# Rows of V with their ones column at a pitch of 272 bytes instead of 260 in a fused attention and MLP kernel

One core of a Trainium2 chip. The metric is the device time of one execution in microseconds (us); lower is better.

## The reference, cut to what matters

```python
h = _layernorm(x) * (1 + ca) + sa                 # x: 1 x 2048 x 512
q = (h @ wq) -> 32 heads of 128                   # 8 KV heads, 4 query heads share one
scores = einsum('bhqd,bhkd->bhqk', q, k) * Dh ** -0.5
p = softmax(scores)                               # over 2048 keys
o = einsum('bhqk,bhkd->bhqd', p, v) @ wo
x = x + ga * o
...                                               # then a gated MLP with a spatial product
```

## The kernel before

Attention works on units: one KV group g (8) and one tile j of 128 queries (16). Scores are made transposed, keys on partitions, so that the exponentials can serve as weights (the stationary operand) of the product with V ("PV") without a transpose. V's rows carry a column of ones behind their 128 values; the 129th output column is then the softmax denominator.

```python
DV = DH + 2                                   # 130 elements of bf16: a pitch of 260 bytes
def load_v(g, rows, engine):
    v1 = late.tile([P, NKT, DV], BF16, name="v1")      # NKT = 16 rows in each partition
    nc.gpsimd.memset(v1[:, :, DH:DV], 1.0)             # the ones
    engine.dma_start(out=v1[:, :, 0:DH], in_=rows[:, g])
...
def qk(u, i):                                 # "QK": two matmuls of 512 columns, then the exponential
    ...
    nc.scalar.activation(out=pTs[u][:, 2 * i : 2 * i + 2, :], in_=s_ps..., func=ACT.Exp, scale=...)
...
def pv(u, i):                                 # eight matmuls a call
    ...
    if i % (2 * per) == 0:                    # two heads share one PSUM bank, DV floats apart
        o_pss[u] = bank("o_ps")[:, 0 : 2 * DV].rearrange("p (h d) -> p h d", h=2)
    for kt in range(part * NKT // per, (part + 1) * NKT // per):
        nc.tensor.matmul(
            o_ps[:, hh % 2, 0 : DH + 1],
            lhsT=pTs[u][:, kt, hh * P : (hh + 1) * P],
            rhs=groups[g]["v1"][:, kt, 0 : DH + 1],    # the moving operand: 129 columns of row kt
            start=(kt == 0), stop=(kt == NKT - 1),
        )
...
for it in range(NU + 6):                      # software pipeline: QK of unit it, PV of unit it - 1
    for i in range(NSLOT):                    # 8 "slots" a unit
        qk(it, i); pv(it - 1, i); ...         # and one 512-column matmul of a projection as filler
```

## Time and profile before

| | before |
|---|---|
| median time | 1361.92 us (3 runs, 1361.52 to 1363.76) |
| TensorE (PE) busy | 1318.9 us, 97% of the span |
| ScalarE (ACT) busy | 1079.6 us, 79% |
| attention, first PV to end of the last | 28.3 to 1173.0 us |
| one slot: 8 PV, 2 QK, 1 filler | 1115 ns, 1024 of them |

The prediction shows the lines. In the page's groups a line reads: source line, engine, operation, output<-input, shape, count | busy us, mean ns of one | idle us just before. Matmul records are pipelined and overlap, so the mean duration of a matmul (220 ns for 129 columns) is not what it costs. What it costs is the distance from its start to the start of the next, called its step below.

### The profile page before, as it was taken

How to read it: one execution, taken by the hardware profiler on the slowest of the kernel's cores; microseconds unless marked ns; L12 is line 12 of the kernel's file. 1: busy time of each engine (PE TensorE's matmuls, PEld its weight loads, DVE VectorE, ACT ScalarE, POOL GpSimd, SP SyncE). 2: the span in 40 equal slices, each digit the busy share in tenths (PEclk: the TensorE clock that was granted, in tenths of full speed). 3: DMA queues.
4: the chain of work that ended last, by engine and by line, in shares of the span. 5: the costliest groups of instructions: out<-in, count | busy, mean ns of one | idle time of the engine just before them, and what ended most of it. 6: DMA issues, size and time to landing. Idle time of an engine off the chain costs nothing.

```text
span 1360.8 us, 27642 instructions
## 1 busy us (share of the span) xinstructions
PE 1318.9 (97%) x12137; PEld 873.7 (64%) x12345; DVE 476.7 (35%) x1171; ACT 1079.6 (79%) x1059; POOL 45.5 (3%) x88
## 2 busy tenths in 40 slices
PE   6999999999999999999999999999999999979997
PEld 4666666666666666666666666666666667634444
DVE  5442222222222222222222222222222566872444
ACT  4789999999999999999999999999999999541000
POOL 1010000000000000000000000000000000110000
PEclk9999999999999999999999999999999999989999
DMA  8120021102211120022010310121111121143200
GB/s 270 28 63 16 13 63 36 21 17 33 62 21 21 32 67 17 16 36 66 17 17 17 83 21 17 18 66 32 21 20 17 25 32 32 25 108 78 67 23 26
DMA packets 141183, 56.53 MB, mean 42 GB/s; under 512 B 131104, under 2 KB 136352, under 8 KB 141056
## 3 DMA queue, kind: packets, MB, share of 16 engines
q1 hardware_dynamic: 137504, 42.17, 14.8%
q0 software_dynamic: 3408, 12.45, 3.6%
q8 instruction: 98, 1.61, 0.5%
q14 instruction: 29, 0.24, 0.1%
q10 hardware_dynamic: 144, 0.07, 0.0%
HBM read 21.63 MB, written 2.10 MB: 17 GB/s over the span
## 4 chain that ended last, share of the span: by engine, by line
PE 93%; DVE 3%; SPq 2%; issue 1%; DMA 1%; POOL 0%; ACT 0%; ACTq 0%; POOLq 0%; DVEq 0%
PE o_ps L901 35%; PE s_ps L879 35%; PE misc L843 7%; PE misc L933 6%; PE misc L1205 6%; PE s_ps L1100 2%; SPq L1012 1%; PE o_ps L1220 1%; PE s_ps L1064 1%; DMA wq_g<-in_A_wq_dram 1%; DVE stz L1081 1%; PE misc L796 0%; PE s_ps L1220 0%; DVE hT L803 0%; DVE z L679 0%
## 5 line engine op out<-in xcount | busy, mean ns | idle before, releaser
L886 ACT ACTIVATE pT<-s_ps 128x1024 bf16<-128x1024 f32 x1024 | 1046.0, 1024 | 106.5 <-PE s_ps L879 30.3
L901 PEld LDWEIGHTS <-pT 128*128 128x128 bf16 x8192 | 559.6, 98 | 241.8
L901 PE MATMUL o_ps<-v,pT 128*128 128x129 bf16 x8192 | 646.3, 220 | 0.0
L879 PE MATMUL s_ps<-qT,kT 128*128 128x512 bf16 x2048 | 609.4, 379 | 10.9 <-DVE qT L852 0.8
L912 DVE RECIPROCAL rall<-o_ps 128x2 f32<-128x2 f32 x256 | 43.6, 170 | 765.3 <-PE o_ps L901 765.2
L879 PEld LDWEIGHTS <-kT 128*128 128x128 bf16 x2048 | 196.7, 97 | 121.2 <-issue 1.5
L843 PE MATMUL misc<-hT,wq_g 128*128 128x512 bf16 (+2 forms) x462 | 169.1, 376 | 0.8 <-DMA wq_g<-in_A_wq_dram 0.8
L933 PE MATMUL misc<-wo_g,oT 128*128 128x512 bf16 x386 | 145.7, 377 | 0.0
L913 DVE TENSOR_TENSOR onorm<-o_ps,rall 128x256 bf16<-128x256 f32 x256 | 108.7, 425 | 8.8
L1205 PE MATMUL misc<-wsp,z 128*128 128x512 bf16 (+2 forms) x555 | 100.5, 336 | 1.9 <-DVE gb L1214 1.4
L852 DVE CAST qT<-misc 128x512 bf16<-128x512 f32 (+1 forms) x129 | 87.3, 676 | 1.7 <-PE misc L843 1.7
L1205 PEld LDWEIGHTS <-z 128*128 128x128 bf16 x560 | 50.6, 98 | 50.4 <-issue 1.9
L946 DVE TENSOR_TENSOR xacc<-misc,xacc 128x512 f32<-128x512 f32 x112 | 76.2, 680 | 0.0
L843 PEld LDWEIGHTS <-wq_g 128*128 128x128 bf16 x528 | 52.2, 100 | 4.0 <-issue 1.5
L933 PEld LDWEIGHTS <-oT 128*128 128x128 bf16 x512 | 50.3, 98 | 0.7
L1214 DVE TENSOR_TENSOR gb<-misc,bsp_bc 128x512 bf16<-128x512 f32 (+2 forms) x35 | 20.4, 584 | 60.9 <-PE misc L1205 60.9
L1100 PE MATMUL s_ps<-hT,win_sb 128*128 128x512 bf16 x109 | 27.2, 408 | 7.3 <-ACT z1T L1108 7.1
L1108 ACT ACTIVATE z1T<-s_ps 128x1024 bf16<-128x1024 f32 x14 | 14.2, 1024 | 20.1 <-PE s_ps L1100 11.6
L1064 PE MATMUL s_ps<-win_sb,hT 128*128 128x448 bf16 x128 | 27.0, 352 | 0.1
L1074 ACT ACTIVATE z<-s_ps 128x896 bf16<-128x896 f32 x16 | 14.7, 917 | 15.0 <-PE s_ps L1064 15.0
L1100 PEld LDWEIGHTS <-win_sb 128*128 128x128 bf16 x112 | 11.6, 103 | 22.5 <-issue 11.0
L712 POOL MEMSET v<- 128x32 bf16 x8 | 1.0, 127 | 715.7 <-issue 615.0
(68 smaller groups left out, 288.8 us busy)
## 6 DMA issues: line engine op xcount, KB each, us to landing
v<-in_A_v_cache_dram POOLq DMA_DIRECT2D x7, 512.0 KB, 6.7
wo_g<-in_A_wo_dram POOLq DMA_DIRECT2D x7, 512.0 KB, 4.8
wq_g<-in_A_wq_dram POOLq DMA_DIRECT2D x7, 512.0 KB, 6.0
wsp<-in_w_mod_dram SPq DMA_DIRECT2D x1, 2048.0 KB, 9.3
oT<-onorm SPq DMA_TRANSPOSE x128, 2.4
out_dram<-yout SPq DMA_DIRECT2D x15, 128.0 KB, 1.7
win_sb<-in_B_w_in_dram SPq DMA_DIRECT2D x1, 1792.0 KB, 13.7
wmod_a<-in_w_mod_dram SPq DMA_DIRECT2D x1, 1024.0 KB, 5.5
```

The costliest lines, as they stand in the source:

```text
L843: nc.tensor.matmul(ps[0][:, o0 : o0 + n], lhsT=wqs[g][:, dt, hh * DH : (hh + 1) * DH], rhs=hTs[ch][:, dt, c0 : c0 + n], start=(dt == 0), s ...
L852: nc.vector.tensor_copy(out=qTs[b][:, hs[0] : hs[-1] + 1, c0 : c0 + n], in_=ps[0][:, 0 : len(hs) * n].rearrange("p (h q) -> p h q", q=n),)
L879: nc.tensor.matmul(s_ps[:, h * 512 : (h + 1) * 512].rearrange("p (r q) -> p r q", r=REP), lhsT=groups[g]["kT"][:, kt * P : (kt + 1) * P], ...
L886: nc.scalar.activation(out=pTs[u][:, 2 * i : 2 * i + 2, :], in_=s_ps[:].rearrange("p (k q) -> p k q", k=2), func=ACT.Exp, scale=inv_sqrt_dh,)
L901: nc.tensor.matmul(o_ps[:, hh % 2, 0 : DH + 1], lhsT=pTs[u][:, kt, hh * P : (hh + 1) * P], rhs=groups[g]["v1"][:, kt, 0 : DH + 1], start=( ...
L912: nc.vector.reciprocal(out=rall[:, c0 : c0 + 2], in_=o_ps[:, :, DH])
L913: nc.vector.tensor_tensor(out=onorms[u][:, hh - 1 : hh + 1, :], in0=o_ps[:, :, 0:DH], in1=rall[:, c0 : c0 + 2].unsqueeze(2).to_broadcast([ ...
L933: nc.tensor.matmul(X_ps[:], lhsT=oTs[u][:, hh, :], rhs=groups[g]["wo"][:, hh, :], start=(hh == 0), stop=(hh == REP - 1),)
L946: nc.vector.tensor_tensor(out=xaccs[j][:], in0=X_ps[:], in1=xaccs[j][:], op=ALU.add)
L1064: nc.tensor.matmul(ps[0][:, hf * 512 : hf * 512 + FC], lhsT=h2Ts[j // CT][:, dt, (j % CT) * P : (j % CT + 1) * P], rhs=win_sb[:, dt, FH + ...
L1100: nc.tensor.matmul(ps[0][:, k * 512 : (k + 1) * 512], lhsT=win_sb[:, dt, f * P : (f + 1) * P], rhs=h2Ts[2 * ch2 + k][:, dt, :], start=(dt ...
L1205: nc.tensor.matmul(g_ps[:, :n], lhsT=z2[:, st, f * P : (f + 1) * P], rhs=wsp[t][:, st, c0 : c0 + n], start=(st == 0), stop=(st == NT - 1),)
```

## The change

Its intent: let every row of V begin at a multiple of 16 bytes. The same constant also spaces the two heads in PSUM (520 to 544 bytes) and widens the memset of the ones.

```diff
-    DV = DH + 2
+    DV = DH + 8
```

## The prediction

> **What bounds the kernel now.** I read the page first (busy shares, slices, costliest groups), then the windows, to see whether TensorE ever stops, then the timeline of one period, and last the start times of single matmuls.
>
> ```profile
> PE 1318.9 (97%) x12137; PEld 873.7 (64%) x12345; DVE 476.7 (35%) x1171; ACT 1079.6 (79%) x1059; POOL 45.5 (3%) x88
> ...
> L886 ACT ACTIVATE pT<-s_ps 128x1024 bf16<-128x1024 f32 x1024 | 1046.0, 1024 | 106.5 <-PE s_ps L879 30.3
> L901 PEld LDWEIGHTS <-pT 128*128 128x128 bf16 x8192 | 559.6, 98 | 241.8
> L901 PE MATMUL o_ps<-v,pT 128*128 128x129 bf16 x8192 | 646.3, 220 | 0.0
> L879 PE MATMUL s_ps<-qT,kT 128*128 128x512 bf16 x2048 | 609.4, 379 | 10.9 <-DVE qT L852 0.8
> ```
>
> TensorE is busy for 97% of the span. The third group, L901, is the product of the probabilities with V: 8192 matmuls that stream one row of V and its ones column, 129 columns of bf16. The changed pitch is the pitch of exactly that operand. The engine was never idle in front of it (0.0). ScalarE, which computes the exponentials (L886), has the second largest load.
>
> ```profile
> 300.00:600.00 300.00, 297.28 (x2912) 204.34 (x2961) 79.92 (x201) 275.52 (x270) 5.58 (x8) 1.00 0.16 33
> 600.00:900.00 300.00, 297.32 (x2913) 204.33 (x2961) 79.92 (x201) 275.52 (x270) 6.87 (x10) 1.00 0.17 34
> ```
>
> These are windows (length, then busy us and count of PE, PEld, DVE, ACT, POOL, then the granted clock and DMA). In attention, PE is busy 99% of the time at full clock, so whatever one matmul gives up shortens the run by itself.
>
> ```profile
> 600.70 0.63 PE L901 MATMUL o_ps<-v,pT 128*128 128x129 bf16 x8
> ...
> 601.16 0.38 PE L843 MATMUL misc<-hT,wq_g 128*128 128x512 bf16 x1
> ...
> 601.38 0.59 PE L879 MATMUL s_ps<-qT,kT 128*128 128x512 bf16 x2
> ...
> 601.81 0.63 PE L901 MATMUL o_ps<-v,pT 128*128 128x129 bf16 x8
> ...
> 1352.34 1.06 PE L1205 MATMUL misc<-wsp,z 128*128 128x128 bf16 x16
> ```
>
> The timeline (start, length, both in us) shows one period, a "slot": 8 PV matmuls, one 512-column matmul of filler, 2 QK matmuls, and 1.11 us later the next 8. There are 8192/8 = 1024 slots, and 1024 x 1.115 = 1142 us is the attention stretch of 28 to 1173 us. Eight PV matmuls take 0.63 us, of which the last one's modelled pipeline is 0.22 (the mean on the page), so seven steps take 0.41: 58.6 ns a step. The last line is my control: 16 matmuls of 128 columns from rows that all start at a multiple of 16 bytes, each with its own weight load as well: (1.06 - 0.22)/15 = 56.0 ns a step. One column more would account for 0.4 ns of the difference of 2.6.
>
> So I took the start of every PV matmul from the trace and sorted the steps by the index kt of the V row (means of 512 each; kt 7 and 15 end a slot, and the median of theirs is 59 to 60):
>
> ```
> kt          0    1    2    3    4    5    6  |   8    9   10   11   12   13   14
> kt*260 %16  0    4    8   12    0    4    8  |   0    4    8   12    0    4    8
> step, ns  56.7 60.9 59.1 59.1 55.9 59.3 59.2 | 56.7 60.9 59.2 59.1 55.9 59.1 59.3
> ```
>
> The period is four, and it is that of 260 modulo 16. The V tile starts at a multiple of 32 bytes in the built program, so rows with kt a multiple of 4 start at a multiple of 16 bytes. Those are the fast ones.
>
> **What the Trainium skill says.** "TensorE: Matmul & The Clock Gate", section "Back-to-back issue gap", gives the isolated gap of a warm matmul as N/2.4 + 2.5 ns: 56.25 for 129 columns. The trace agrees for aligned rows (56.7 and 55.9, mean 56.3) and for 512 columns (215.8 by the formula, 215 measured); unaligned rows take about 3 ns more. The same section states a sustained 81 ns for N=128 with weight loads; this trace does not agree (56 for the control, 59 for PV). "SBUF — State Buffer", section "Specifications (TRN2)", says that lines are of 16 bytes and that crossing to a new line costs something. A row of 258 bytes touches 17 lines at offset 0, 4, 8 or 12 alike, so the page points at 16 bytes but does not by itself give this cost. Its section "Operand start alignment" says its alignment rule "is about legality, not speed"; the trace shows that here there is a speed too.
>
> **The change part by part.** No instruction is added, removed or moved: the order of each engine is the same, and only the shapes of the 8 memsets differ.
>
> (a) Pitch of V, 260 to 272 bytes. 272 is 17 x 16, and the tile's base in the changed program is again a multiple of 32, so all 16 rows start as kt 0, 4, 8 and 12 do now. A slot's eight steps now: 56.7 + 60.9 + 59.1 + 59.1 + 55.9 + 59.3 + 59.2 and 59.5 into the next matmul (mean of those steps) = 469.7 ns. After: 8 x 56.25 = 450.0. Saved: 19.7 ns a slot, all on the engine that sets the end; 1024 slots give 20.2 us. The coarse reading agrees: (58.6 - 56.4) x 8192 = 18 us.
>
> (b) What takes part of it back. In the last four tiles of attention (1133 to 1165 us) four of eight slots have no filler; there the exponentials start every 904 ns, against 430 + 470 = 900 ns of PE work, so ScalarE is level with PE. Those 16 slots may save nothing: 16 x 19.7 = 0.3 us lost.
>
> (c) The same constant sets the pitch of the two heads in PSUM, 520 to 544 bytes. I expect nothing: the step is the same for both heads of a bank now (kt 0: 56.8 and 56.7), though the second starts at byte 520.
>
> (d) Memsets of V's tail grow from 128x32 to 128x128 elements. Eight of 0.13 us each, on POOL, which is 3% busy and fills V tens of us ahead: nothing on the path. Writes of V rows by DMA: the same sizes, and 14.8% + 3.6% of DMA share now.
>
> (e) After attention nothing changes; it starts 20 us earlier. Sum: 1361.9 - 20.2 + 0.3 = 1342.0 us, 1.5% less.
>
> **The rivals.**
>
> 1. ScalarE becomes the bound. For: 1024 ns of activation in a slot of 1115, which will be 1095, and 79% busy. Against: where nothing holds it back it starts every 904 ns, its records overlapping; its queue starts 1114 apart now because PE does. It would have to floor at 1100 to take a quarter of the gain (1347 us). I give that 4%.
>
> 2. Weight loads become the bound. For: each PV matmul has a load of 98 ns, and fast steps now come one in four, so a slow neighbour might lend it time. Against: the control sustains 56 ns for 16 matmuls in a row with a load each. Should loads hold the average at 57.5, the gain is halved (1352 us). 5%.
>
> 3. The period of four has another cause. The weights of PV lie 1024 bytes apart in kt, which also repeats after four where 4096 counts. Against: these addresses move by 256 bytes from head to head, and the pattern does not; all of them are multiples of 16. Then the change does nothing: 1362 us. 6%.
>
> 4. A row at a multiple of 16 ends with one element alone on its seventeenth line, and the skill wants two hits a line. But the fast rows of today end in just that way.
>
> 5. PSUM banks, operands or loads come too late for a faster PE. Loads of V, wq and wo land in 5 to 7 us and are issued tens of us early. QK needs a score bank that ScalarE has read: two slots of 1095 = 2190 ns against 0.59 + 1.02 plus hand-overs. No bind.
>
> **Range and chances.** The main case carries about 85%; within it the step may settle at 55.9 (23 us saved, 1339) or 56.7 (16.5 us, 1345). Repeats of before spread over 2.2 us. Range for 8 in 10: 1337 to 1349. Over 2% faster needs 27 us, that is 3.3 ns from each of 8192 matmuls, to 55.4 ns a step, below 129/2.4 + 2.5: 3%. Nothing got slower in the program: 1%. Within 2%: 96%.
>
> **What would show it right or wrong.** Right: eight PV matmuls in 0.61 us in the timeline (7 x 56.25 + 218); L901's busy time at 1024 x 0.612 = 627 us; its spread of durations narrower than 217/220/223, with the median near 218; exponentials 1095 ns apart; ScalarE's idle time up by some 20 us, and its busy time the same; the end of PV at about 1153 us instead of 1173; the MLP part as long as before. Wrong: a pattern of four in kt that stays (rival 3), equal steps at 57 to 59 (rival 2), or fast PV steps with new idle time in front of QK (rival 1 or 5).

## The result

| | before | changed |
|---|---|---|
| median, us | 1361.72 (4 runs) | 1347.0 (4 runs, 1346.54 to 1349.33) |
| ratio | | 0.9893, 95% interval 0.9875 to 0.9910 |
| slot, mean | 1115.2 ns | 1100.8 ns |
| end of the last PV matmul | 1172.98 us | 1158.12 us |
| from there to the end | 187.8 us | 187.1 us |

A ratio is the mean time of one kernel's fast runs over that of the other's of the same rounds, so not quite the ratio of the medians. The time lies in the predicted range, the change is within 2% as forecast, and the place is the predicted one: of 15.5 us by which the profiled span fell, 14.9 were gone by the end of PV.

The page of the changed kernel, the same groups as in the prediction:

```profile
PE 1303.1 (97%) x12137; PEld 860.4 (64%) x12345; DVE 476.3 (35%) x1171; ACT 1079.2 (80%) x1059; POOL 46.4 (3%) x88
...
L886 ACT ACTIVATE pT<-s_ps 128x1024 bf16<-128x1024 f32 x1024 | 1045.6, 1024 | 92.2 <-PE s_ps L879 16.5
L901 PEld LDWEIGHTS <-pT 128*128 128x128 bf16 x8192 | 548.5, 98 | 241.2
L901 PE MATMUL o_ps<-v,pT 128*128 128x129 bf16 x8192 | 631.4, 220 | 0.0
L879 PE MATMUL s_ps<-qT,kT 128*128 128x512 bf16 x2048 | 609.9, 379 | 10.8 <-DVE qT L852 0.8
```

L901 lost 14.9 us of busy time (646.3 to 631.4). The other matmul groups are as they were, ScalarE is as busy as before in a shorter span, and PE still never waits in front of PV. The windows of the changed kernel, columns as before (length, then PE, PEld, DVE, ACT, POOL):

```profile
300.00:600.00 300.00, 297.32 (x2950) 203.59 (x3000) 81.12 (x204) 279.13 (x274) 7.11 (x10) 1.00 0.16 33
600.00:900.00 300.00, 297.32 (x2949) 203.49 (x2998) 81.12 (x204) 279.15 (x273) 7.26 (x10) 1.00 0.18 34
```

PE is as busy as before (297.3 of 300 us), and gets 2950 matmuls done where it got 2912. A busy share could not have told this gain; a count does. The timeline of the changed kernel, successive slots:

```profile
600.76 0.62 PE L901 MATMUL o_ps<-v,pT 128*128 128x129 bf16 x8
...
601.86 0.62 PE L901 MATMUL o_ps<-v,pT 128*128 128x129 bf16 x8
...
602.96 0.62 PE L901 MATMUL o_ps<-v,pT 128*128 128x129 bf16 x8
```

Eight PV matmuls take 0.62 us (0.63 before) and slots start 1.10 us apart. The view of line L901 by itself (duration ns min/median/max), first of before, then of the changed kernel, shows that all of them have become alike:

```profile
L901 PE MATMUL o_ps<-v,pT x8192: 217/220/223, 28.3 to 1172.8; 128*128 128x129 bf16 x200
```

```profile
L901 PE MATMUL o_ps<-v,pT x8192: 218/220/220, 28.1 to 1157.9; 128*128 128x129 bf16 x200
```

The starts of single matmuls, from the trace, give the mean step of each of a slot's eight positions (KV group 2), and of the 512-column matmuls:

```
position      0    1    2    3    4    5    6    7  | 512 columns | slot
before      56.7 60.8 59.2 59.2 55.8 59.3 59.3 59.5 |   215.24    | 1115.4
changed     56.7 56.7 56.7 56.7 56.7 56.7 56.7 56.7 |   215.83    | 1100.8
```

So all eight are now equal, as predicted, but at 56.67 ns and not at 56.25; and the 512-column matmuls have become 0.6 ns slower each. Both are looked into below.

### The profile page after: what moved, and what is told of

The parts are those of the page before. It is cut to its first block, busy times and chain, and to the rows that moved or that the text cites. A ratio compares the mean times of both kernels' runs of the same rounds, so it can differ in the third digit from the quotient of the medians.

```text
span 1345.2 us, 27642 instructions
## 1 busy us (share of the span) xinstructions
PE 1303.1 (97%) x12137; PEld 860.4 (64%) x12345; DVE 476.3 (35%) x1171; ACT 1079.2 (80%) x1059; POOL 46.4 (3%) x88
## 4 chain that ended last, share of the span: by engine, by line
PE 92%; DVE 3%; SPq 2%; issue 1%; DMA 1%; POOL 0%; ACT 0%; ACTq 0%; POOLq 0%; DVEq 0%
PE s_ps L879 35%; PE o_ps L901 34%; PE misc L843 7%; PE misc L933 6%; PE misc L1205 6%; PE s_ps L1100 2%; SPq L1012 1%; PE o_ps L1220 1%; PE s_ps L1064 1%; DMA wq_g<-in_A_wq_dram 1%; DVE stz L1081 1%; DVE hT L803 0%; PE s_ps L1220 0%; PE misc L796 0%; DVE bnst L690 0%
## 5 line engine op out<-in xcount | busy, mean ns | idle before, releaser
L886 ACT ACTIVATE pT<-s_ps 128x1024 bf16<-128x1024 f32 x1024 | 1045.6, 1024 | 92.2 <-PE s_ps L879 16.5
L901 PEld LDWEIGHTS <-pT 128*128 128x128 bf16 x8192 | 548.5, 98 | 241.2
L901 PE MATMUL o_ps<-v,pT 128*128 128x129 bf16 x8192 | 631.4, 220 | 0.0
L879 PEld LDWEIGHTS <-kT 128*128 128x128 bf16 x2048 | 199.8, 98 | 120.1 <-issue 1.3
L1108 ACT ACTIVATE z1T<-s_ps 128x1024 bf16<-128x1024 f32 x14 | 14.2, 1024 | 19.5 <-PE s_ps L1100 10.9
L1074 ACT ACTIVATE z<-s_ps 128x896 bf16<-128x896 f32 x16 | 14.7, 917 | 14.9 <-PE s_ps L1064 14.9
```

The lines of the kernel that those rows point to most:

```text
L879: nc.tensor.matmul(s_ps[:, h * 512 : (h + 1) * 512].rearrange("p (r q) -> p r q", r=REP), lhsT=groups[g]["kT"][:, kt * P : (kt + 1) * P], ...
L901: nc.tensor.matmul(o_ps[:, hh % 2, 0 : DH + 1], lhsT=pTs[u][:, kt, hh * P : (hh + 1) * P], rhs=groups[g]["v1"][:, kt, 0 : DH + 1], start=( ...
```

## The experiments

A new theory arose after the first four runs, so the order of the runs matters. Theory A is that of the prediction: a row that does not start on a 16-byte line costs. Several kernels do something different in each KV group, so that one trace compares up to eight settings, each over some 100 slots. In the tables a slot is the mean of a group's slots of usual length (the few with a stall or without a filler are left out), and steps are means by position. The step at a position runs from that matmul's start to the next one's, so a slow row is one whose own step is long. Diffs are cut to the lines that matter. In the order below, the first seven kernels took 1350.49, 1353.12, 1357.73, 1347.06, 1360.97, 1360.0 and 1352.83 us, one execution each, beside 1361.35 us for one of before.

**The same pitch, the rows shifted off the line.** All rows of group g start 2g bytes past a line.

```diff
-        v1 = late.tile([P, NKT, DV], BF16, name="v1")
+        v_raw = late.tile([P, NKT * DV + 16], BF16, name="v1")
+        v1 = v_raw[:, g : g + NKT * DV].rearrange("p (k d) -> p k d", d=DV)
```

> The changed kernel (pitch 272 bytes), but the V tile of KV group g starts 2*g bytes past its base, so that all 16 rows of one group share one offset from a 16-byte line: 0, 2, 4 ... 14 bytes for the 128 slots of group 0 to 7. Theory A (a row that doesn't start on a 16-byte line costs a fixed amount): steps of 56.7 ns in group 0 and about 59.2 in all of groups 1 to 7, with no pattern of four left in kt; slots of 1101 ns in group 0 and about 1117 in the others. Rival B (what counts is how much of the first line is left, or whether the start is a multiple of 4 or 8): steps grow with the offset, or 4, 8 and 12 bytes are cheaper than 2, 6, 10 and 14. Rival D (the period of four in the kernel before came from the addresses of the probabilities, not of V): 56.7 in every group, or a pattern of four that stays.

```
offset, bytes    0      2      4      6      8      10     12     14
slot, ns      1100.8 1107.5 1100.8 1107.5 1100.8 1107.5 1100.8 1107.4
step 1-7, ns   56.7   57.5   56.7   57.5   56.7   57.5   56.7   57.5
```

Theory A falls here. Rows at 4, 8 and 12 bytes are as fast as rows at 0, though in the kernel before rows at just those offsets took 59 to 61 ns. An odd number of elements costs 0.83 ns a step, which is another and smaller effect (the second form of rival B); no row of the kernel before starts at one. At odd numbers position 0 stays at 56.5 to 56.7 and the 512-column matmul behind the eight takes 216.5 to 216.8 instead of 215.8, so that the slot pays for all eight. Rival D, which expects 56.7 everywhere, is not settled here; the moved base below tests it. The line of PV in the group at 4 bytes has the same single duration as in the changed kernel:

```profile
L902 PE MATMUL o_ps<-v,pT x876: 220/220/220, 329.8 to 450.0; 128*128 128x129 bf16 x176
```

**Eight pitches.**

```diff
+        pitch = (129, 130, 132, 134, 136, 138, 140, 144)[g]
+        v_raw = late.tile([P, NKT * 144], BF16, name="v1")
+        v1 = v_raw[:, 0 : NKT * pitch].rearrange("p (k d) -> p k d", d=pitch)
...                                           # the memset of the ones as wide as the pitch asks
```

> The pitch of V's rows is 258, 260, 264, 268, 272, 276, 280 and 288 bytes in KV groups 0 to 7, base at a multiple of 32, PSUM pitch as in the change. Theory A: of 16 rows those at a multiple of 16 are 2, 4, 8, 4, 16, 4, 8, 16; slots (8 PV, 2 QK, 1 filler matmul) then take about 1117, 1115, 1110, 1115, 1101, 1115, 1110 and 1101 ns, the fast rows being the aligned ones. Rival (272 is good because rows are longer apart, or because 32-byte lines matter): 276, 280 and 288 as fast as 272, or 288 faster than 272.

```
pitch, bytes   slot    steps by position
258           1120.0   56.3 61.0 59.0 59.5 59.4 59.4 59.1 59.5
260           1116.6   56.6 60.9 59.2 59.2 55.8 59.6 59.4 60.4
264           1108.3   56.7 60.8 55.8 59.4 55.9 59.4 55.9 59.1
268           1105.0   56.7 60.5 55.8 56.0 56.5 60.9 55.6 55.6
272           1100.8   56.7 in all
276           1100.8   56.7 58.3 55.8 55.8 56.7 58.3 55.8 55.8
280           1101.1   56.7 59.2 55.8 56.3 55.8 58.6 55.8 56.8
288           1100.8   56.7 in all
```

Theory A missed again: it gave 268 bytes the slot of 260 (1115), and 276 too; they took 1105.0 and 1100.8. Its rival, that rows farther apart are faster, fits the slots, which fall as the pitch grows, but not the single rows: at 264 rows 1 and 2 both start 6 bytes behind the end of the row before, and only row 1 is slow (60.8 and 55.8). At 268 bytes only row 1 of rows 1, 2 and 3 is slow, though all three start off a line.

The table suggests what theory A had mistaken. Count in lines of 16 bytes. At 268, row 0 covers bytes 0 to 257 and ends in line 16 (bytes 256 to 271); row 1 starts at 268, in that same line. Row 1 ends at byte 525, in line 32, and row 2 starts at 536, in line 33. At 264, rows 1, 3, 5 and 7 start in the line in which the row before ended; at 260 all rows do so but 0 and 4; at 258 all but row 0; from 272 up none can. Up to 268 these are the slow rows of the table, without exception. **Theory L**: a matmul is slow when it starts in the 16-byte line in which the matmul just before it ended. A unit of 8 bytes would not do: at 264 row 0 ends in bytes 256 to 263 and row 1 starts at 264, yet row 1 is slow. Nor would one of 32: at 272 row 0 ends and row 1 starts within bytes 256 to 287, and is fast. The lone 58.3 and 59.2 at 276 and 280 are no such rows; they are made good by steps of 55.8 behind them, and the slots lose 0 to 0.3 ns. Why they arise stays open.

**More columns, on the line.**

```diff
-                rhs=groups[g]["v1"][:, kt, 0 : DH + 1],
+                rhs=groups[g]["v1"][:, kt, 0 : DH + 1 + g],
```

> The changed kernel, but the PV matmul of KV group g streams 129+g columns (more copies of the ones column), all rows on a 16-byte line. It asks why an aligned step is 56.67 ns and not the 56.25 that I predicted. Theory P (columns are taken two at a time): 129 and 130 cost the same, [...]56.67 ns; 131 and 132 57.5; 133 and 134 58.3; 135 and 136 59.2. Rival Q (a constant that is larger than 2.5 ns): a step grows by 0.42 ns with each column, 56.67 at 129, 57.1 at 130, 59.6 at 136. Rival R (the 17th line is fetched whole): 129 to 136 cost the same.

```
columns     129   130   131   132   133   134   135   136
step, ns   56.67 56.67 57.50 57.50 58.33 58.33 59.17 59.17
```

Theory P is right to the digit: columns count in pairs, so 129 costs as much as 130. That is 0.42 ns a matmul more than I had predicted.

**Some rows shifted by 4 bytes, at a pitch of 288.**

```diff
+        v1 = late.tile([P, NKT, 144], BF16, name="v1")
...                                           # rows with kt % 8 < g are also loaded 2 elements later
-                rhs=groups[g]["v1"][:, kt, 0 : DH + 1],
+                rhs=groups[g]["v1"][:, kt, (2 if kt % 8 < g else 0) :][:, 0 : DH + 1],
```

> Pitch 288 bytes, but of the eight rows of a slot the first g (group g, 0 to 7) start 4 bytes past a 16-byte line, the others on it. It asks why a slot won 14 ns and not 19.7, and what an unaligned row costs alone. Theory A with additive cost: slots of 1101 ns plus a constant 2.4 ns for each unaligned row (1103, 1106 ... 1118 for 7). Rival S (slack: the 512-column matmuls, 215.0 ns apart in the kernel before and 215.8 now, and aligned rows of 55.9 make up part of an unaligned row's cost): the first one or two unaligned rows cost nothing (slot 1101), the later ones about 3 ns each. Which positions are slow: A says the shifted ones alone.

All eight groups took 1100.8 ns a slot and 56.7 ns a step, with 0 to 7 shifted rows. Both of the theories that it was to tell apart fell with theory A: an unaligned row costs nothing when it shares no line.

Theory L was now stated, and the next three kernels were made to break it.

**Columns until the row reaches the next one's line.** Pitch 272, all rows 4 bytes past a line, 129 + g columns (the first and the third edit together, the first with a fixed 2 elements).

```diff
+        v1 = v_raw[:, 2 : 2 + NKT * DV].rearrange("p (k d) -> p k d", d=DV)
-                rhs=groups[g]["v1"][:, kt, 0 : DH + 1],
+                rhs=groups[g]["v1"][:, kt, 0 : DH + 1 + g],
```

> Pitch 272 bytes, all rows 4 bytes past a 16-byte line, 129+g columns in KV group g. Theory L (formed from the first runs: a matmul is slow when its first 16-byte line is the line that the matmul just before it ended in; where the row starts is free): a row of 129 to 134 columns ends before the line of the next row's start, so groups 0 to 5 take what they took with aligned rows (slots of 1101, 1101, 1108, 1108, 1114, 1114 ns); with 135 and 136 columns the row runs 2 and 4 bytes into the line in which the next row starts, so seven of eight matmuls are slow and slots go from 1121 to about 1140 ns. Theory A (the start off a line costs) is refuted already if groups 0 and 1 take 1101; a theory that only the number of lines touched counts expects 134 and 135 columns to differ in another place, from 134 columns on 17 to 18 lines at 135, by less than 1 ns a step.

```
columns    129    130    131    132    133    134    135    136
slot     1100.8 1100.8 1107.5 1107.5 1114.2 1114.2 1138.3 1138.3
step 0     56.7   56.7   57.5   57.5   58.3   58.3   59.2   59.1
steps 1-7  56.7   56.7   57.5   57.5   58.3   58.3   62.0   62.0
```

The jump comes where theory L put it, between 134 and 135 columns. One column more ends the row not at byte 271 but at 273 counted from the line below its start, in the line where the next row starts. Only position 0 of a slot, which follows a 512-column matmul, stays at the pace of 135 columns on the line (59.2). The timeline of this kernel shows it in both places, 1.11 and 1.14 us apart:

```profile
780.75 0.63 PE L902 MATMUL o_ps<-v,pT 128*128 128x134 bf16 x8
...
781.86 0.63 PE L902 MATMUL o_ps<-v,pT 128*128 128x134 bf16 x8
...
920.77 0.66 PE L902 MATMUL o_ps<-v,pT 128*128 128x135 bf16 x8
...
921.91 0.65 PE L902 MATMUL o_ps<-v,pT 128*128 128x135 bf16 x8
```

**Pitch 260, the base moved.**

```diff
+        v_raw = late.tile([P, NKT * DV + 16], BF16, name="v1")
+        b0 = 2 * (g % 4)
+        v1 = v_raw[:, b0 : b0 + NKT * DV].rearrange("p (k d) -> p k d", d=DV)
```

> The kernel before (pitch 260), with the base of the V tile 0, 4, 8, 12 bytes past a line in groups 0 to 3, and again in 4 to 7. Theory L: the unshared rows move with the base. Slow rows of a slot (index in the slot): 1,2,3,5,6,7 at base 0 (slot 1115 ns); 1,2,4,5,6 at base 4; 1,3,4,5,7 at base 8; 2,3,4,6,7 at base 12 (slots of 1110 to 1113). The first row of a slot comes after 512-column matmuls and is fast at every base, though at bases 4, 8 and 12 row 8 shares a line with row 7. Rival D (addresses of the probabilities) expects rows 0 and 4 fast at every base; theory A expects row 0 slow at bases 4, 8 and 12.

```
base, bytes   slot    steps by position                          slow as expected
0            1115.5   56.6 60.8 59.2 59.2 55.8 59.3 59.3 59.4    1 2 3 5 6 7
4            1113.3   56.7 60.8 59.2 55.8 59.6 59.5 59.2 55.8    1 2 4 5 6
8            1111.7   56.7 60.8 55.8 59.8 59.2 59.1 55.9 59.4    1 3 4 5 7
12           1113.3   56.7 56.7 60.8 59.6 59.6 55.8 60.0 59.2    2 3 4 6 7
```

Every slow position is the expected one; groups 4 to 7 repeat them. Position 0, which theory A expected to be slow at bases 4, 8 and 12, is fast. The pattern moves with the base of V while the addresses of the probabilities follow no such shift, so rival D (rival 3 of the prediction) is out. Row 8, at position 0, shares a line with row 7 at the last three bases and is fast: two or three other matmuls came between.

**No padding, another order of use.**

```diff
-        for kt in range(part * NKT // per, (part + 1) * NKT // per):
+        seq = ((0, 1, 2, 3, 4, 5, 6, 7), (7, 6, 5, 4, 3, 2, 1, 0),
+               (0, 2, 4, 6, 1, 3, 5, 7), (0, 1, 4, 5, 2, 3, 6, 7))[g % 4]
+        for n, k in enumerate(seq):
+            kt = part * NKT // per + k
...
+                start=(part == 0 and n == 0), stop=(part == per - 1 and n == len(seq) - 1),
```

> The kernel before, pitch 260 and no padding at all; only the order in which the eight rows of a slot are used changes by KV group: 0 and 4 natural; 1 and 5 reversed; 2 and 6 even rows first, then odd; 3 and 7 the order 0,1,4,5,2,3,6,7. Theory L: natural 1115 ns a slot; reversed and even-odd 1101, all steps near 56.7, since no matmul starts in the line in which the one before it ended; the last order has its second, fourth, sixth and eighth matmul slow and takes about 1108, as pitch 264 did. Rival L2 (any line that the matmul before has read costs, whichever end it is at): reversed is slow as well, since a row ends in the line where the one before it began. Theory A (starts off a line): 1115 in every group.

```
order              slot    steps by position
0 1 2 3 4 5 6 7   1115.3   56.7 60.8 59.2 59.1 55.9 59.3 59.4 59.4
7 6 5 4 3 2 1 0   1101.7   56.7 56.7 56.7 56.7 60.0 55.8 55.9 55.8
0 2 4 6 1 3 5 7   1101.7   56.7 59.2 55.8 55.9 55.8 60.0 55.9 55.8
0 1 4 5 2 3 6 7   1108.7   56.6 60.8 55.8 59.2 55.8 59.5 55.8 59.6
```

The same rows at the same addresses are slow or fast by what came just before them. Reversed order is fast, so rival L2 is out in the form tried: a matmul that ends in the line in which the one before began is not slow (56.7 and 55.8; row 3, the one of 60.0, ends in no such line). A matmul that starts in a line which the one before read earlier than its end was not tried. In the last order positions 1, 3, 5 and 7 are slow, as expected. Lone long steps in the two fast orders (60.0 for row 3, 59.2 for row 2 with even rows first) are made good by the 55.8 behind them to within 0.9 ns a slot; why they arise stays open. Slots of this kernel with even rows first, at a pitch of 260, start 1.10 us apart like those of the changed kernel:

```profile
330.96 0.62 PE L908 MATMUL o_ps<-v,pT 128*128 128x129 bf16 x8
...
332.06 0.62 PE L908 MATMUL o_ps<-v,pT 128*128 128x129 bf16 x8
...
333.16 0.62 PE L908 MATMUL o_ps<-v,pT 128*128 128x129 bf16 x8
```

The four kernels that follow were timed together, in three rounds on one chip; before took 1361.81 us there (7 runs).

**Half of the change: V's pitch alone.** PSUM heads stay 520 bytes apart.

```diff
-            o_pss[u] = bank("o_ps")[:, 0 : 2 * DV]...
+            o_pss[u] = bank("o_ps")[:, 0 : 2 * (DH + 2)]...
```

> Half of the change: V rows at 272 bytes, the two heads in PSUM still 520 bytes apart. If all of the gain comes from V's rows: 1347 us, ratio 0.989 to before. If the PSUM pitch matters (theory C), less gain.

1347.44 us, ratio 0.9893 (0.9877 to 0.9910).

**The other half: the PSUM pitch alone.** V at 260 bytes, heads 544 bytes apart.

```diff
-            o_pss[u] = bank("o_ps")[:, 0 : 2 * DV]...
+            o_pss[u] = bank("o_ps")[:, 0 : 2 * (DH + 8)]...      # DV = DH + 2
```

> The other half: V rows at 260 bytes, the heads in PSUM 544 bytes apart. Gain from V's rows alone: 1361.5 us, ratio 1.000; at most 1.5 us slower, since a group with this pair of pitches had slots of 1116.6 instead of 1115.2 ns. Theory C (PSUM pitch): up to 14 us faster.

1362.0 us, ratio 1.0005 (0.9988 to 1.0022), slots of 1115.2 ns. The gain is all V's; theory C is out. The 1116.6 ns that one group took at this pair of pitches above did not come back, so the PSUM pitch alone does not make it; what does stays open.

**No padding, even rows first, everywhere.**

```diff
+        seq = (0, 2, 4, 6, 1, 3, 5, 7)
```

> The kernel before with no padding, the eight rows of each slot used in the order 0,2,4,6,1,3,5,7. Theory L (shared line between successive matmuls): the whole gain without the change, 1347 us, ratio 0.989, and steps near 56.7. Theory A (start off a 16-byte line): 1361.5 us, ratio 1.000.

1349.93 us (1348.93 to 1350.39), ratio 0.9910 (0.9893 to 0.9926). A kernel that never touched the pitch wins 11.9 us where the change wins 14.4: most of the gain, where theory L had foretold the whole. Its slots are 0.9 ns longer than those of the changed kernel, which makes 0.9 us. In its profiled run, the slowest of the four, another 1.8 us went at the start of attention (PV began 0.5 us later, and its first two slots took 2.15 and 1.38 us instead of 1.10), where the granted clock dropped (windows of this kernel, the column after PE is the clock):

```profile
26.00:28.00 2.00, 1.20 (x11) 0.99 1.03 404
28.00:30.00 2.00, 2.00 (x12) 0.50 0.23 90
30.00:32.00 2.00, 1.95 (x13) 0.66 0.00 0
32.00:34.00 2.00, 2.00 (x23) 1.00 0.00 0
```

The changed kernel had 1.00 throughout there, and 22 matmuls in 28 to 30 us. Whether all of this kernel's runs met that stretch, its one profile cannot say.

**The change again**, in the same rounds, unedited.

> The change itself on the same chip and in the same rounds, to set the three beside it: 1347 us, ratio 0.989.

1347.37 us, ratio 0.9892 (0.9876 to 0.9909). No kernel of the study beats it by more than the spread of its own runs (1346.72 to 1347.73).

## Why the prediction was right or wrong

The time was in the range, the saving was some way off (20.2 us forecast, 14.7 measured), and the reason given for it was wrong. That the range held is luck: a pitch of 272 takes away both the start off a line, which costs nothing here, and the line shared with the row before, which was the cost.

- **What bounds the kernel.** Right. PE had no slack in attention, and what PV gave up came off the end.
- **Reading of the pattern of four.** Here the prediction failed. The sentence "rows with kt a multiple of 4 start at a multiple of 16 bytes. Those are the fast ones" is true of the kernel before, and I took it for the cause. At a pitch of 260 the rows on a line are also those that do not start in the line where their predecessor ended; one pitch with one base cannot tell the two apart. Rows at 4, 8 and 12 bytes are fast at 272; unpadded rows are fast in another order; and at 272 with a shifted base rows turn slow when they grow by one column into the next row's line. With it falls the sentence that the start alignment has a speed here: for rows that start at an even number of elements none was found (slots of 1100.8 ns at 0, 4, 8 and 12 bytes). Why a shared line costs is not shown, only when.
- **Part (a), the size.** The mechanism as a sum over a slot was right, two terms were mis-sized. The aligned step was put at 56.25 ns from a formula; it is 56.67, since columns count in pairs: 8 x 0.417 = 3.3 ns a slot. And nothing was set against the 512-column matmuls, which took 215.16 ns before (mean of the groups) and 215.83 now: 3 x 0.67 = 2.0 ns. 19.7 - 3.3 - 2.0 = 14.4 ns, the measured 1115.2 - 1100.8; times 1024 it is 14.7 us. In a stretch held up by slow rows, other matmuls run a little closer (215.0 for 512 columns, 55.8 for a fast row) and make up part of the loss, so the slow rows cannot be summed alone. Counted per slow row, a slot loses 2.1 ns with two of them (4.2/2, pitch 268), 1.9 with four (7.5/4, pitch 264), 2.4 with six (14.4/6), 2.7 with seven (19.2/7, pitch 258). Counted instead from the closer pace, 8 x 55.83 + 3 x 215.0 = 1091.7 ns a slot, the loss is nearly the same for each slow row wherever four or more keep the stretch held up: 4.2 ns (16.6/4), 3.9 (23.5/6) and 4.0 (28.3/7). With two it is not (13.3/2): there the 512-column matmuls are back at 215.8 on average. I had seen the fast steps at 55.9 and 56.7 and averaged them, where the kernel settled on the slower one; the prediction had named that case (56.7, 16.5 us saved).
- **Part (b).** Right: in the slots without filler the four starts before were 0.90 us apart each, and are now 0.88, 0.88, 0.91 and 0.92 us apart, as much in sum.
- **Parts (c), (d), (e).** Right: the PSUM pitch alone gives 1.0005; the memsets grew from 127 to 205 ns each, off the path; the MLP part took as long to within 0.7 us.
- **Rivals.** ScalarE, weight loads and late buffers did not bind: PE's idle time before PV is 0.0, all eight steps are equal, and with more columns and the same loads they follow the columns (56.67 to 59.17). Rival 1 had named the very outcome, a floor at 1100 ns and 1347 us, and that is a coincidence: the slot is the sum of PE's own steps, 8 x 56.67 + 3 x 215.83 = 1100.8 ns, and in slots without filler the exponentials of the changed kernel still start 904 ns apart. The true alternative, that successive rows share a line, was not on my list, and it foretells the same time for this change.
- **What was to be seen.** Right in direction and short of the numbers: 0.62 us and not 0.61, 631.4 and not 627, exponentials 1101 ns apart and not 1095, PV over at 1158 and not 1153. The durations did close up, but at 220 and not 218. One sign was wrong: I expected ScalarE's idle time to rise by 20 us, and it fell from 106.5 to 92.2, because its work stayed the same and the span shrank.

## What to carry to other kernels

Where matmuls in a row stream short rows that lie one behind the other, let no row start in the 16-byte line in which the last one ended (shown here for rows of 129, 135 and 136 bf16 columns in one kernel): round the pitch up so that a line's boundary lies between, or use the rows in another order; where the first row starts does not matter, so long as it is an even number of bf16 elements. Read this from start-to-start times, since busy share and mean duration hardly move. And when a pattern in one layout has two readings, vary the base at a fixed pitch and the order at fixed addresses before believing either: this prediction had a good number with the wrong reason behind it, and the reason would have misled at a pitch of 276.

## What the Trainium skill lacked or had wrong

- No page has the shared line. "SBUF — State Buffer" (section "Specifications (TRN2)") says that each crossing to a new line of 16 bytes pays, which no run here isolates. What paid here is another case: a matmul that starts in the line in which the one before ended took 59 to 61 ns instead of 56.7 (62.0 instead of 59.2 at 135 columns), while rows that start 4, 8 or 12 bytes inside a line of their own cost nothing (slots of 1100.8 ns at all of them).
- The same page, section "Operand start alignment", speaks of legality alone. In speed, a moving operand of 129 columns that starts at an odd bf16 element takes 57.5 ns instead of 56.7.
- "TensorE: Matmul & The Clock Gate", section "Back-to-back issue gap", gives N/2.4 + 2.5 ns. It holds for even N (56.67 at 130, 59.17 at 136, 215.8 at 512); odd N costs as much as N + 1 (56.67 at 129, where the formula has 56.25).
- The same section's 81 ns for sustained matmuls of 128 columns with weight loads is not met here: 16 in a row ran 56 ns apart, and those of 129 columns at 56.67 in every KV group of the changed kernel.
